# Fifteen short loads in the load queue, between two pieces of W_down

## The chip, the cores and the metric

The kernel runs on one core of a Trainium2 chip. The time is device time in microseconds (us), the median of several runs. A core has five engines with instruction streams of their own: TensorE (PE, matrix products; its weight loads are shown apart as PEld), VectorE (DVE), ScalarE (ACT), GpSimd (POOL) and SyncE (SP). SP computes nothing here. It issues transfers, which 16 DMA engines carry out. A transfer signals its end through a semaphore.

## The reference

One decode step of a transformer block, for a batch of 4 with one token each, in bfloat16. `x` is 4 x 576.

```
h  = x + Attention(layernorm(x))
h2 = h + MLP(layernorm(h))

Attention: q = x @ wq                     32 heads of 128
           k, v = the last 4096 rows of the caches, 16 heads (each serves 2 query heads)
           softmax(q k^T / sqrt(128)) v, then @ wo
MLP:       gate = x @ W_gate; up = x @ W_up      (576 x 4608)
           (gate where gate > 0) * up, then @ W_down   (4608 x 576)
```

Nearly all bytes are the K and V windows (128 MiB); the weights are another 24 MB.

## The kernel before, in words

The program is written as a list of operations per engine (`Prog`, `P.op`, `P.dma`); each names the operations it depends on, and `emit` turns these into semaphore waits. Each engine's list is executed in the order in which it was written.

All large loads are issued by SP, in one queue. `place` puts a load into a region of one SBUF tile (`arena`) and makes it wait for the readers of what was there before. The order is: `wq`; the K and V tiles, 16 of each, 4 MiB each, in a ring of four slots; `wo`; `W_gate` in two pieces; `W_up` in three; and `W_down` in five pieces (line 282). `WD_ROWS` = 0, 15, 25, 32, 35, 36 are the borders of these: W_down is held as 36 rows of 576 on each of 128 partitions, and piece 1 has rows 0 to 14, piece 2 rows 15 to 24, piece 3 rows 25 to 31, piece 4 rows 32 to 34, and piece 5 row 35. So a partition gets 17280, 11520, 8064, 3456 and 1152 bytes.

The K and V phase transposes each K tile on DVE (line 422), multiplies it with q on PE (lines 446 and 34), takes the softmax, and multiplies with V (lines 507 and 34). Then follow `wo`, the second layer norm, gate and up (line 664), and the product with W_down (line 685), which runs through the 36 rows in order, waiting for a piece where it begins. The result is copied out of PSUM by DVE (line 701) and ACT (line 702), and stored by two small transfers, one from SP and one from ACT (line 706). SP's last operation waits for both.

The regions of the five W_down pieces were used by K and V tiles; the last reader of these is a product with V, after which SP can issue all five.

Of the kernel before, what the change touches and what calls it, by code (L numbers as in the profile page):

```python
# [9 lines left out]
BF16 = mybir.dt.bfloat16  # L10
# [110 lines left out]
def bass_sequential_preLN__sliding_block_cached__glu_gated_reglu__decode_kernel(  # L121
# [12 lines left out]
    with ExitStack() as es:  # L134
        cnt = [0]

        def sb(name, shape, dt):
            return es.enter_context(nc.sbuf_tensor("sb_" + name, shape, dt))

        P = Prog()  # L140
# [48 lines left out]
        st2 = sb("st2", [128, 40], FP32)  # L189
        tmp5 = sb("tmp5", [128, DC, B], FP32)  # L190
        out_sb = sb("out_sb", [128, 352], BF16)


        pT = pp[:, 0:4096]
# [21 lines left out]
        def place(name, off, size, reader, make, key=None):  # L216
            deps = []
            for blk in range(off // 64, (off + size) // 64):
                r = owner.get(blk)
                if r is not None and r not in deps:  # L220
                    deps.append(r)
                owner[blk] = reader
            semk = key or "d_" + "_".join(str(v) for v in name)
            P.dma("sync", ("L",) + name, make, semk, deps)
            land[name] = off
# [19 lines left out]
        def main_rows(W):  # L245
            return W[0:512, :].rearrange("(p r) n -> p (r n)", r=4)
# [22 lines left out]
        for g, W in ((0, B_W_gate), (1, B_W_up)):  # L269
            for m, n, src in ((4, F // 2, last_rows(W)), (0, 3 * F, main_rows(W)[:, 0:3 * F]), (3, F, main_rows(W)[:, 3 * F:4 * F])):  # L270
                if g == 0 and m == 0:
                    n, src = 4 * F, main_rows(W)
# [7 lines left out]
        for r0, r1 in zip(WD_ROWS, WD_ROWS[1:]):  # L280
            place(("wd", r0), wd_off + r0 * D, (r1 - r0) * D, ("DOWN", 1),
                  lambda e, r0=r0, r1=r1: e.dma_start(  # L282
                      out=arena[:, wd_off + r0 * D:wd_off + r1 * D],
                      in_=B_W_down.rearrange("(p r) n -> p (r n)", p=128)[:, r0 * D:r1 * D]))


        pool("c_eps", lambda e: e.memset(eps_c[:, :], EPS))
# [15 lines left out]
                                                in_=c_qm[:, :, :].rearrange("p q (h j) -> p q h j", j=4),  # L303
# [4 lines left out]
                                                in_=to_v[:, :, :].rearrange("p n (k a) -> p n k a", a=4),  # L308
# [14 lines left out]
        for sg in range(2):  # L323
            pool(f"c_toq{sg + 1}", lambda e, sg=sg: e.affine_select(
                out=toq[:, :, :, :], in_=toq[:, :, :, :],
# [213 lines left out]
        def finish_o():  # L539
            for q in range(4):  # L540
                for qd in range(4):
# [17 lines left out]
                                              in_=bass.AP(tensor=e8, offset=0, ap=[[8, 128], [0, 4], [1, 8]])), ["c_e8", "c_selc0"])  # L559
# [47 lines left out]
        for a in range(8):  # L607
            for n in range(2):
                for j in range(4):
# [4 lines left out]
                    else:  # L614
# [6 lines left out]
                                             in_=bass.AP(tensor=psb, offset=512 + 224, ap=[[4096, 128], [1, 64], [0, 2]])), ["part1"])  # L621
# [54 lines left out]
        for i in range(2):  # L676
            dve(("HHT", i), lambda e, i=i: e.transpose(
                out=hhT[:, 576 * i:576 * i + 576].rearrange("p (r q) -> p r q", q=32),
                in_=bass.AP(tensor=pp, offset=3712 + 18 * i, ap=[[PPW, 128], [1, 18], [36, 32]])), [("HH", m) for m in range(3)])
# [24 lines left out]
        for n in range(2):  # L704
            lo, hi = ncol[n]
            P.dma(("sync", "scalar")[n], ("O", n), lambda e, n=n, lo=lo, hi=hi: e.dma_start(
                out=orow[:, lo:hi], in_=out_sb[32 * n:32 * n + 4, 0:hi - lo]),
                "d_out", [f"OUT{n}"])
        P.op("sync", None, None, [("O", n) for n in range(2)])
        P.emit(nc, es)  # L710


# [26 lines left out]
```

## Time and profile before

| | |
|---|---|
| time, median of 3 runs | 378.55 us (377.77 to 378.62) |
| profiled execution, span from the first to the last instruction | 376.5 us |
| what the median has above that span | 2.05 us |
| DVE busy | 227.6 us (60%) |
| PE busy | 209.2 us (56%) |
| read from HBM | 159.58 MB, 424 GB/s over the span |
| W_down pieces issued | 337.4 to 339.6 us |
| first product with W_down | 367.0 us |
| mean granted clock of TensorE | 0.791 |

The profiled execution has no time of its own beside its span, so the median is used for what lies around the span. A page of the profile shows the busy share of each engine in 40 equal slices of the span as digits (9 is 90% or more), the rows of the DMA queues (packets, MB, and the share of 16 engines' time), and the chain of work that ended last, followed back from the last instruction. In a timeline, a row has its start, its length, the engine, the line of the kernel, the operation, its output and inputs, and in brackets how long the engine had been idle and what ended that. The trace also has a record for every packet that a DMA engine moved, with its start, its duration and its size; a packet of 4 bytes is a write to a semaphore.

### The profile page before, as it was taken

The page shows a single profiled execution, that of the slowest core. Times are in us where ns is not written, and L with a number is a line of the kernel's source. Part 1 is how long each engine was busy: PE and PEld are TensorE (multiplying, and loading weights), DVE is VectorE, ACT ScalarE, POOL GpSimd, SP SyncE. Part 2 cuts the span into 40 slices and gives each one's busy share as a digit, 9 for nine tenths or more (in the row PEclk, how much of TensorE's full clock was granted, in tenths as well). Part 3 has the DMA queues.
Part 4 walks back from the last instruction along what each step waited for, and adds up shares of the span by engine and source line. Part 5 has one row for each costly group of instructions (what it writes and reads, how often), then busy time and mean ns, then how long its engine had stood idle before and what let it go on. Part 6 is the DMA issues. An engine that isn't in the chain of part 4 may idle for free.

```text
span 376.5 us, 2541 instructions
## 1 busy us (share of the span) xinstructions
PE 209.2 (56%) x1447; PEld 39.2 (10%) x694; DVE 227.6 (60%) x164; ACT 53.8 (14%) x84; POOL 10.7 (3%) x29
## 2 busy tenths in 40 slices
PE   0404443249919091749282844664555687776748
PEld 0000000001101010101010100110000101003305
DVE  3088878779292959584847778665659423342140
ACT  3093000211000114010101140101010401121010
POOL 8300000000000000000000000000000000000000
PEclk9975666659979687788778885968596989996688
DMA  8999999999999999999999999999999999999996
GB/s 335 446 435 432 413 446 446 425 411 446 444 421 414 443 444 421 414 446 446 421 413 446 446 418 421 438 446 418 425 439 446 413 432 435 430 423 426 437 414 263
DMA packets 6514, 159.74 MB, mean 424 GB/s; under 512 B 736, under 2 KB 872, under 8 KB 1512
## 3 DMA queue, kind: packets, MB, share of 16 engines
q1 hardware_dynamic: 6488, 159.58, 98.8%
q8 instruction: 8, 0.13, 0.1%
q10 hardware_dynamic: 16, 0.01, 0.0%
q14 instruction: 2, 0.02, 0.0%
HBM read 159.58 MB, written 0.00 MB: 424 GB/s over the span
## 4 chain that ended last, share of the span: by engine, by line
DMA 62%; DVE 18%; PE 18%; SPq 1%; issue 1%; ACT 0%
DMA sb_arena<-in_A_k_cache_dram 53%; DVE sb_arena L422 16%; PE psb L34 11%; DMA sb_arena<-in_B_W_down_dram 9%; PE psb L446 4%; PE psb L507 2%; DVE sb_o_tmp L520 1%; DVE sb_pp L485 1%; PE psb L685 0%; SPq L242 0%; PE psb L473 0%; SPq L282 0%; ACT sb_out_sb L702 0%; SPq L255 0%; SPq L251 0%
## 5 line engine op out<-in xcount | busy, mean ns | idle before, releaser
L422 DVE STREAM_TRANSPOSE sb_arena<-sb_arena 128x8192 f32<-128x8192 f32 (+1 forms) x19 | 139.9, 7365 | 66.5 <-DMA sb_arena<-in_A_k_cache_dram 66.5
L446 PE MATMUL psb<-sb_arena 128*32 128x512 bf16 x256 | 42.5, 629 | 119.1 <-DVE sb_arena L422 119.0
L34 PE MATMUL psb<-sb_arena,sb_pp 128*128 128x512 bf16 x382 | 105.2, 383 | 2.7 <-issue 2.6
L507 PE MATMUL psb<-sb_arena,sb_pp 128*128 128x512 bf16 x115 | 44.1, 383 | 8.9 <-DVE sb_o_tmp L520 8.9
L34 PE MATMUL psb<-sb_arena 128*32 128x512 bf16 x256 | 44.2, 649 | 0.0
L517 ACT COPY sb_o_tmp<-psb 32x512 f32<-32x512 f32 x32 | 18.5, 577 | 179.3 <-PE psb L34 179.1
L520 DVE TENSOR_TENSOR sb_o_tmp<-psb,sb_fm 32x512 f32<-32x512 f32 x32 | 21.7, 678 | 16.9 <-PE psb L34 16.4
L446 PEld LDWEIGHTS psb<-sb_arena 128*32 128x32 bf16 x256 | 9.6, 119 | 161.4 <-DVE sb_arena L422 132.2
L507 PEld LDWEIGHTS psb<-sb_arena,sb_pp 128*128 128x128 bf16 x128 | 12.6, 99 | 113.4 <-issue 113.4
L524 DVE TENSOR_REDUCE sb_o_sel<-sb_o_tmp 128x128 f32<-128x512 f32 x16 | 17.7, 1106 | 0.5
L465 ACT ACTIVATE sb_pp<-psb,sb_hx 128x1024 bf16<-128x1024 f32 x4 | 4.5, 1113 | 78.4 <-DVE sb_hx L462 78.4
L485 DVE TENSOR_TENSOR sb_pp<-psb,sb_m 128x1024 bf16<-128x1024 f32 x8 | 9.4, 1209 | 4.5 <-PE psb L473 4.5
L480 ACT ACTIVATE sb_pp<-psb,sb_m 128x512 bf16<-128x512 f32 x16 | 9.7, 692 | 14.8 <-PE psb L473 14.8
L523 DVE TENSOR_TENSOR sb_o_tmp<-sb_o_tmp,sb_fm 64x512 f32<-64x512 f32 x16 | 11.0, 690 | 0.5
L413 ACT COPY sb_arena<-sb_q_keep 32x256 bf16<-32x256 bf16 x8 | 9.7, 1452 | 0.1
L685 PE MATMUL psb<-sb_arena,sb_pp 128*32 128x352 bf16 (+1 forms) x72 | 7.6, 349 | 3.7 <-DMA sb_arena<-in_B_W_down_dram 3.6
L399 DVE CAST sb_pp<-psb 128x512 bf16<-128x512 f32 x1 | 2.4, 2426 | 11.3 <-PE psb L379 11.3
L468 DVE STREAM_TRANSPOSE sb_pp<-sb_pp 128x1024 bf16<-128x1024 bf16 x4 | 5.0, 1246 | 5.1 <-ACT sb_pp L465 5.1
L473 PE MATMUL psb<-sb_pp,sb_to_v 128*32 128x256 bf16 x64 | 4.3, 401 | 6.2 <-DVE sb_pp L468 6.2
L673 DVE TENSOR_TENSOR sb_pp<-psb,sb_pp 128x384 bf16<-128x384 f32 x3 | 1.5, 551 | 9.0 <-PE psb L664 9.0
L379 PE MATMUL psb<-sb_arena,sb_xnT 128*32 128x512 bf16 x16 | 2.6, 628 | 7.2 <-DMA sb_arena<-in_A_wq_dram 7.2
L664 PE MATMUL psb<-sb_arena,sb_hnT 128*32 128x384 bf16 x40 | 4.2, 405 | 3.9 <-DVE sb_hnT L645 2.0
(119 smaller groups left out, 88.1 us busy)
## 6 DMA issues: line engine op xcount, KB each, us to landing
sb_arena<-in_A_k_cache_dram SPq DMA_DIRECT2D x16, 4096.0 KB, 26.2
sb_arena<-in_A_v_cache_dram SPq DMA_DIRECT2D x16, 4096.0 KB, 28.5
sb_arena<-in_A_wo_dram SPq DMA_DIRECT2D x1, 4608.0 KB, 26.2
sb_arena<-in_B_W_gate_dram SPq DMA_DIRECT2D x1, 4608.0 KB, 29.3
sb_arena<-in_A_wq_dram SPq DMA_DIRECT2D x1, 4096.0 KB, 12.9
sb_arena<-in_B_W_up_dram SPq DMA_DIRECT2D x1, 3456.0 KB, 30.3
sb_arena<-in_B_W_down_dram SPq DMA_DIRECT2D x1, 2160.0 KB, 29.6
sb_arena<-in_B_W_down_dram SPq DMA_DIRECT2D x1, 1440.0 KB, 32.6
```

What stands on the lines that cost most here:

```text
L34: return e.add_instruction(mybir.InstMatmult(name=e.bass.get_next_instruction_name(), engine=mybir.EngineType.PE, ins=[e.lower_ap(rhs), e. ...
L413: act("QW", lambda e, i=i, q=q: e.copy(out=bass.AP(tensor=arena, offset=32 * i * AW + 2 * i + q, ap=[[AW, 32], [512, 16], [136, 4], [32, 4]]),
L422: dve(("TRA", g), lambda e: e.transpose(out=dst, in_=src), [("L", "K", g)] if lo == 0 else [])
L446: fn = lambda e, out_=out_, lhsT=lhsT, rhs=rhs, start=start, stop=stop: e.matmul(out_, lhsT=lhsT, rhs=rhs, start=start, stop=stop, skip_gr ...
L480: act(("EV", b, 0), lambda e, a=a: e.activation(out=bass.AP(tensor=pp, offset=2 * a, ap=[[PPW, 128], [8, 2], [32, 128], [1, 2]]), in_=bank ...
L485: dve(("EV", b, 1), lambda e, n=n: e.tensor_tensor(out=bass.AP(tensor=pp, offset=16 + 8 * n, ap=[[PPW, 128], [32, 128], [2, 4], [1, 2]]), ...
L507: fn = lambda e, lhsT=lhsT, rhs=rhs, k=k, j=j: e.matmul(bank[2 + j], lhsT=lhsT, rhs=rhs, start=(k == 0), stop=(k == 7), skip_group_check=True)
L517: act(("OSC", g), lambda e, j=j: e.copy(out=o_tmp[32 * j:32 * j + 32, 0:512], in_=bank[2 + j][32 * j:32 * j + 32, :]), [("PV", g), ("OSEL" ...
L520: dve(("OSD", g), lambda e, j=j: e.tensor_tensor(out=ot(32 * j, 32), in0=bank[2 + j][32 * j:32 * j + 32, :].rearrange("p (t d) -> p t d", ...
L523: dve(("OS", g), lambda e: e.tensor_tensor(out=ot(64, 64), in0=ot(64, 64), in1=fmb(64, 64), op=ALU.mult), [("OSC", g)])
L524: dve(("OSEL", g), lambda e: e.tensor_reduce(out=o_sel[:, qd, b, :], in_=o_tmp[:, 0:512].rearrange("p (t d) -> p d t", d=DH), axis=AX.X, o ...
L685: return lambda e: e.matmul(bank[n][32 * n:32 * n + 32, 0:hi - lo], lhsT=lhsT, rhs=w[:, lo:hi], start=start, stop=stop, skip_group_check=True)
```

## The change

After the load of the piece that begins at row 15, SP issues fifteen more loads. Load k takes the first 40 + k elements (bfloat16) of the first k rows of `wq`, and writes them to k partitions, eight apart, of a new scratch tile, `mark`. Nothing reads that tile. All fifteen count on one semaphore, and SP's last wait also waits for the fifteenth. The three remaining pieces of W_down are issued after them.

```
         out_sb = sb("out_sb", [128, 352], BF16)
+        mark = sb("mark", [128, 1024], BF16)
...
         for r0, r1 in zip(WD_ROWS, WD_ROWS[1:]):
             place(("wd", r0), ...)
+            if r0 == 15:
+                for k in range(1, 16):
+                    P.dma("sync", ("L", "mark", k), lambda e, k=k: e.dma_start(
+                        out=bass.AP(tensor=mark, offset=64 * k, ap=[[8 * 1024, k], [1, 40 + k]]), in_=A_wq[0:k, 0:40 + k]), "d_mark")
...
-        P.op("sync", None, None, [("O", n) for n in range(2)])
+        P.op("sync", None, None, [("O", n) for n in range(2)] + [("L", "mark", 15)])
```

## The prediction

> **What bounds the kernel now.** I read the page first, for the engines and the DMA row.
>
> ```profile
> span 376.5 us, 2541 instructions
> ...
> DMA  8999999999999999999999999999999999999996
> GB/s 335 446 435 432 413 446 446 425 411 446 444 421 414 443 444 421 414 446 446 421 413 446 446 418 421 438 446 418 425 439 446 413 432 435 430 423 426 437 414 263
> ...
> q1 hardware_dynamic: 6488, 159.58, 98.8%
> ...
> q10 hardware_dynamic: 16, 0.01, 0.0%
> ```
>
> The DMA engines are busy in all 40 slices, and 98.8% of their time belongs to q1, the queue that SP fills. No compute engine is busy for more than 60% of the span. So the time is that of 159.58 MB through one queue, and a change matters if it lengthens what stands in q1 or lets q1 run dry. Next, the chain of work that ended last, cut to the end, shows what follows the last bytes:
>
> ```profile
> 338.19 0.04 issue
> 338.23 34.60 DMA sb_arena<-in_B_W_down_dram
> 372.83 0.04 issue
> 372.88 1.86 PE psb L685 x19
> 374.74 0.02 issue
> 374.76 0.44 ACT sb_out_sb L702
> ```
>
> The third W_down piece is issued at 338.23 and lands at 372.83. Its 34.6 us are almost all waiting behind older transfers. After it come 1.86 us of PE and a copy. The timeline of the same stretch has the waits:
>
> ```profile
> 337.39 2.23 SPq L282 DMA_DIRECT2D sb_arena<-in_B_W_down_dram  x5
> ...
> 372.88 0.86 PEld L685 LDWEIGHTS psb<-sb_arena,sb_pp 128*32 128x32 bf16 x14 [0.48 <-DMA sb_arena<-in_B_W_down_dram]
> 373.95 0.45 PEld L685 LDWEIGHTS psb<-sb_arena,sb_pp 128*32 128x32 bf16 x8 [0.21 <-DMA sb_arena<-in_B_W_down_dram]
> 374.62 0.38 DVE L701 CAST sb_out_sb<-psb 32x224 bf16<-32x224 f32 x1 [8.34 <-PE psb L685]
> 374.76 0.44 ACT L702 CAST sb_out_sb<-psb 32x352 bf16<-32x352 f32 x1 [15.56 <-PE psb L685]
> 375.03 0.34 SPq L706 DMA_DIRECT2D out_dram<-sb_out_sb  x1
> ```
>
> SP issues all five pieces in 2.23 us. PE waits 0.48 us for piece 3 and 0.21 us for piece 4. Whatever delays the arrival of piece 4 delays the end by as much. Last, the list of issues:
>
> ```profile
> sb_arena<-in_B_W_down_dram SPq DMA_DIRECT2D x1, 2160.0 KB, 29.6
> sb_arena<-in_B_W_down_dram SPq DMA_DIRECT2D x1, 1440.0 KB, 32.6
> ...
> sb_arena<-in_B_W_down_dram SPq DMA_DIRECT2D x1, 1008.0 KB, 34.6
> ...
> sb_arena<-in_B_W_down_dram SPq DMA_DIRECT2D x1, 432.0 KB, 35.2
> sb_arena<-in_B_W_down_dram SPq DMA_DIRECT2D x1, 144.0 KB, 35.1
> ```
>
> Every piece waits about 30 us: the backlog at that point.
>
> **The change part by part.** The diff puts the fifteen loads behind the piece of rows 15 to 24, so they stand between the second and the third of the five pieces. Nothing is removed. PE, DVE, ACT and POOL keep their instructions in order. SP gets 15 issues and one wait.
>
> *Issue on SP.* The pieces follow one another at 0.47 us (2.23 us for five). Other rows for an issue are 0.33 us (the first piece, in the chain) and 0.56 us (the 4-row load of x on ACT). Fifteen cost 7.1 us, between 5.0 and 8.4. Piece 3 is then issued at 338.2 + 7.1 = 345.3 instead of 338.2, and piece 5 at 346.3. The trace's packet records show the first engine finishing its share of piece 2 at 368.2. The first load of the run was issued at 0.80 and had its first packet at 1.85, so 1.05 us are needed ahead. The cover is 368.2 - 1.05 - 346.3 = 20.8 us, and the issue costs nothing. Nobody else waits on SP: its next work is the output at 375.0. If this cover were gone, q1 would run dry ahead of piece 3.
>
> *Data in q1.* The loads have 1 + 2 + ... + 15 = 120 rows of 82 to 110 bytes, 12 KB together; by bytes alone, at 424 GB/s, 0.03 us. Per packet it is more. The packet records of the W_down pieces are straight in size:
>
> ```
> 3456-byte packets 135 ns, 1152-byte packets 51 ns (next one starts after 47),
> 4-byte semaphore packets 9 ns (next one starts after 6)
> ```
>
> That is 9 ns plus 0.0365 ns per byte, so a row takes 12 to 13 ns, of which 4 overlap with the next. A row and its semaphore packet add 8.5 + 6 = 14.5 ns to an engine's stream, or 21.5 without overlap. q10 in the page carried two transfers of 4 rows in 16 packets, 4 rows and 4 semaphore packets each, so I take one engine per row. Then one engine gets 15 rows, the next 14, and the last none. The longest stream grows by 15 x 14.5 = 0.22 us, at most 0.32. If instead some of these loads put all their rows on one engine, that engine has at most 120 x 8.5 + 15 x 6 = 1.1 us more.
>
> *Does it reach the end?* The engines finish unevenly: the semaphore packets of piece 2 lie between 368.19 and 369.99, ten of the sixteen in the last 0.63 us. If the busiest engine for these loads is a late one, the end moves by the full 0.22 us. If the six engines with the most rows are just the six early ones, a late engine still has up to 9 rows, 0.13 us. I take 0.2 us, between 0 and 1.1.
>
> *The last wait.* SP also waits for the fifteenth load, long landed. A step between SP instructions is 0.04 us in the chain; I take 0.04.
>
> *More code on SP.* Fifteen more instructions could fetch one more piece of code. Pieces of 16 KB took 1.0 to 1.1 us of one DMA engine in this trace while sharing it, about 0.6 us by its 27 GB/s (32768 bytes in 1.216 us). I take 0, bound 0.6, since SP has few instructions.
>
> *What the trace cannot show* is a dense row of small transfers in one queue. The nearest rows: pieces 4 and 5 are 1.08 and 0.38 us long per engine, and their packets stand without a gap. So a transfer does not wait for the one before it to be confirmed, at least at a spacing of 0.38 us. Confirmation takes longer than that: the last semaphore packet of piece 5 is at 373.85 and the semaphore is counted at 374.26, 0.41 us. A spacing of 15 ns is not shown by any row. So a load costs an engine 0.015 us if semaphore writes run on, and at most about 0.4 us if each waits for the one before. I take the low end, because no gap is there at 0.38 us, and keep 15 x 0.4 = 6 us as the high end. A gain has no source: packets already run at their fixed durations.
>
> Sum: 0 + 0.2 + 0.04 + 0 = 0.25 us. The page gives the profiled span, 376.5 us; the median of the timed runs, 378.55, lies 2.05 above it, and I leave that as it is. 378.55 + 0.25 = 378.8.
>
> **Rules of the Trainium skill against these rows.** "DMA: Bandwidth & Descriptors", Anatomy of one DMA, gives a fixed cost of about 2.0 us for every transfer, and its Rules for kernel authors say that transfers under 64 KB pay mostly overhead. Charged to the queue one by one that would be an estimated 15 x 2.0 = 30 us, the rule that speaks loudest against this change. The gapless pieces 4 and 5 say that the fixed part is latency and not occupancy, at their size. The same page calls the bubble of a semaphore write tiny, which sides with the 6 ns row. Its section on why a DMA increments its semaphore by 16 says that a transfer of k rows takes the lowest-numbered k engines; no row here shows which.
>
> **Rivals.**
> - *Confirmations line up (slower).* Fifteen semaphore writes stand close together on one engine, and each holds the next until it is confirmed. For: 0.41 us from packet to count, and no row with a closer spacing than 0.38 us. Against: no gap at 0.38 us. Price: up to 15 x 0.4 = 6 us on the engine with 15 rows; if that one is 1.4 us ahead of the last, 4.6. Time 383 to 384.5. A partial form (0.1 to 0.2 us each, a read that is not fetched far enough ahead) gives 1.5 to 3 us, 380 to 381.5. It decides from 0.08 us per load (1.14 / 15).
> - *The queue holds only so many transfers (slower).* At 339 nine transfers are outstanding and SP issues at its normal pace. With the change it would be 24. If there is a limit near 16, SP is held until small loads drain, after 370. Piece 3 then starts about 1.05 us late plus the issues of pieces 4 and 5, 2 x 0.47: 2.0 us, 380.6. Against: the nine are 81 descriptors per engine, without a stall; the fifteen add only 30 at most.
> - *Hidden altogether.* The early engines carry the rows and the late ones few: 0.05 us, 378.6. It can't be told from my forecast.
> - *Faster.* Only by chance, 377 or less; the runs before span 377.77 to 378.62.
>
> **How the numbers follow.** About 0.3%, 1.14 us, is what a measurement of this kernel can tell from no change. My forecast and the hidden case together, 378.5 to 379.1: 0.60. Confirmations in full: 0.15. Their partial form: 0.12. The limit of the queue: 0.09. A faster run: 0.04. The three slow cases sum to 0.36. The range begins at 377.9, below the hidden case by the spread of the runs, and reaches to 383.0, which takes in the partial form and the limit, and leaves out most of the full form. The likeliest case alone has 378.0 to 379.6.
>
> **What the profile after would show.** Right: q1 with 6488 + 240 = 6728 packets; SP issuing for some 9 us from 337.4; piece 3 with a landing time of about 27.7 us instead of 34.6, because it is issued 7 us later and lands at the same moment; PE's waits for pieces 3 and 4 changed by less than 0.3 us; the DMA row at 9 to the end. Wrong: a wait of PE for piece 3 that has grown from 0.48 us to several us, with the GB/s of slice 39 down (confirmations), or the issue of piece 3 after 360 (limit of the queue). Both would overturn the forecast. Fewer than 240 new packets would mean that rows do not go one to an engine.

## The result, and the profile after

| | before | changed |
|---|---|---|
| time, median of 9 runs | 378.31 us (377.77 to 378.62) | 379.21 us (378.88 to 379.49) |
| ratio | | 1.0024, 95% interval 1.0014 to 1.0034 |
| profiled execution, span | 376.5 us | 378.1 us |

The change costs 0.9 us. The time is inside the stated range, and the loss is within the 0.3% that the prediction called no change; but it is more than three times the 0.25 us of the forecast's sum, and the interval excludes that sum. The two profiled executions are 1.6 us apart, more than the medians. The one shown of before is near its fastest run: its span is 2.05 us below the median that was known then, while the changed kernel's profiled execution took 379.37 us with a span of 378.1, only 1.27 less. And piece 1 of W_down, which lands before any of the new loads has moved, already lands 0.27 us later in the changed kernel's profile (367.27 against 367.00); piece 2 lands 0.36 us later (370.77 against 370.41). That part is taken as a difference between executions.

The page of the changed kernel, engines and queue:

```profile
span 378.1 us, 2556 instructions
...
DMA  8999999999999999999999999999999999999995
GB/s 333 444 444 388 442 444 444 433 399 444 442 437 433 406 439 444 433 413 430 444 439 430 413 437 444 422 437 419 440 440 425 426 430 440 424 433 412 425 427 204
DMA packets 6754, 159.75 MB, mean 423 GB/s; under 512 B 976, under 2 KB 1112, under 8 KB 1752
...
q1 hardware_dynamic: 6728, 159.60, 98.6%
```

The queue has 240 packets more (6488 before), as worked out: 120 rows and 120 semaphore writes. The DMA engines count as busy to the end, so the loss does not show in the DMA row: a packet that is held up counts as a busy engine. The timeline at the end:

```profile
374.53 0.86 PEld L690 LDWEIGHTS psb<-sb_arena,sb_pp 128*32 128x32 bf16 x14 [1.17 <-DMA sb_arena<-in_B_W_down_dram]
...
375.59 0.46 PEld L690 LDWEIGHTS psb<-sb_arena,sb_pp 128*32 128x32 bf16 x8 [0.20 <-DMA sb_arena<-in_B_W_down_dram]
376.26 0.38 DVE L706 CAST sb_out_sb<-psb 32x224 bf16<-32x224 f32 x1 [9.70 <-PE psb L690]
376.40 0.44 ACT L707 CAST sb_out_sb<-psb 32x352 bf16<-32x352 f32 x1 [15.49 <-PE psb L690]
```

PE's wait for piece 3 has grown from 0.48 to 1.17 us; the one for piece 4 is unchanged (0.21, 0.20), and so is what follows. So the loss lies between the landings of pieces 2 and 3. Its chain there:

```profile
351.54 0.80 SPq L288
352.34 0.04 issue
352.38 22.10 DMA sb_arena<-in_B_W_down_dram
374.48 0.04 issue
374.53 1.85 PE psb L690 x19
```

From the landing of piece 2 to that of piece 3 it was 372.83 - 370.41 = 2.42 us; now it is 374.48 - 370.77 = 3.71, 1.29 us more in this execution. The busy times by stretch show when. The first table is of before, the second of the changed kernel. The last number of a row is what the DMA engines moved, in GB/s; ahead of it stand the DMA share and PE's granted clock:

```profile
368.00:370.00 2.00, 2.00 (x20) 1.25 (x17) 0.00 (x0) 0.00 (x0) 0.00 (x0) 0.50 0.98 416
370.00:372.00 2.00, 2.00 (x24) 1.28 (x22) 0.00 (x0) 0.00 (x0) 0.00 (x0) 0.81 0.99 412
372.00:374.00 2.00, 1.88 (x23) 1.12 (x21) 0.00 (x0) 0.00 (x0) 0.00 (x0) 1.00 0.55 213
```

```profile
368.00:370.00 2.00, 2.00 (x21) 1.40 (x17) 0.00 (x0) 0.00 (x0) 0.00 (x0) 0.50 1.07 363
370.00:372.00 2.00, 2.00 (x18) 1.00 (x16) 0.00 (x0) 0.00 (x0) 0.00 (x0) 0.50 0.99 326
372.00:374.00 2.00, 1.72 (x16) 0.87 (x13) 0.00 (x0) 0.00 (x0) 0.00 (x0) 0.89 0.83 329
```

From 368 to 372 the rate falls from 414 to 345 GB/s, while the DMA share stays near 1. (PE's wait grew by only 0.69 us, because PE itself came to piece 3 0.96 us later, at 373.36 instead of 372.40: it began 0.27 us later, and then needed 6.05 instead of 5.36 us for its weight loads of pieces 1 and 2, at a granted clock of 0.50 instead of 0.81 from 370 to 372.) The packet records say what holds the data up. They do not name the engine, so an engine's packets were strung together by their times, each beginning where the one before ends. The new rows are as fast as foreseen: 12 to 13 ns each, a row and its semaphore write every 14 to 15 ns. But of the 128 packets of piece 3 (8064 bytes, every one of them 305 ns before) 19 took more than 400 ns, up to 1576, always the first or the fifth of an engine's eight, and only on engines that had carried about five or more of the new loads. The large packets behind the new loads wait, not the new loads.

### The profile page after: what moved, and what is told of

Its sections match the earlier page's. It is cut to its first block, busy times and chain, and to the rows that moved or that the text cites. A ratio compares the mean times of both kernels' runs of the same rounds, so it can differ in the third digit from the quotient of the medians.

```text
span 378.1 us, 2556 instructions
## 1 busy us (share of the span) xinstructions
PE 210.9 (56%) x1447; PEld 38.7 (10%) x694; DVE 228.7 (60%) x164; ACT 53.8 (14%) x84; POOL 10.5 (3%) x29
## 4 chain that ended last, share of the span: by engine, by line
DMA 54%; PE 21%; DVE 20%; SPq 3%; issue 1%; ACT 0%
DMA sb_arena<-in_A_k_cache_dram 48%; DVE sb_arena L427 16%; PE psb L34 13%; DMA sb_arena<-in_B_W_down_dram 6%; PE psb L451 4%; PE psb L512 3%; SPq L288 3%; DVE sb_o_tmp L525 1%; DVE sb_pp L490 1%; PE psb L478 1%; PE psb L690 0%; DVE sb_pp L473 0%; DVE sb_hx L456 0%; ACT sb_pp L470 0%; SPq L283 0%
## 5 line engine op out<-in xcount | busy, mean ns | idle before, releaser
L34 PE MATMUL psb<-sb_arena,sb_pp 128*128 128x512 bf16 x382 | 107.8, 391 | 3.1 <-issue 3.0
L512 PE MATMUL psb<-sb_arena,sb_pp 128*128 128x512 bf16 x115 | 44.8, 390 | 8.9 <-DVE sb_o_tmp L525 8.9
L485 ACT ACTIVATE sb_pp<-psb,sb_m 128x512 bf16<-128x512 f32 x16 | 9.8, 697 | 14.5 <-PE psb L478 14.5
L34 PE MATMUL psb<-sb_arena,sb_hnT 128*32 128x384 bf16 x80 | 6.2, 394 | 0.0
```

The lines of the kernel that those rows point to most:

```text
L34: return e.add_instruction(mybir.InstMatmult(name=e.bass.get_next_instruction_name(), engine=mybir.EngineType.PE, ins=[e.lower_ap(rhs), e. ...
L485: act(("EV", b, 0), lambda e, a=a: e.activation(out=bass.AP(tensor=pp, offset=2 * a, ap=[[PPW, 128], [8, 2], [32, 128], [1, 2]]), in_=bank ...
L512: fn = lambda e, lhsT=lhsT, rhs=rhs, k=k, j=j: e.matmul(bank[2 + j], lhsT=lhsT, rhs=rhs, start=(k == 0), stop=(k == 7), skip_group_check=True)
```

## The experiments

Three theories were open: A, the engine reads ahead over a fixed number of packets, and short rows fill that; B, the semaphore writes at the end of the loads hold what stands behind them; C, SP is late with pieces 3 to 5. Every time below is compared with before on the same chip, and edits are against the changed kernel. "Gap" is the time from the landing of piece 2 to that of piece 3 in the profile (2.42 us before).

| run | loads | per engine: rows, semaphore writes | ratio (95%) | gap |
|---|---|---|---|---|
| the change | 15 of 1 to 15 rows | 0 to 15 each | 1.0024 (1.0014 to 1.0034) | 3.71 us |
| e1 | the same, behind piece 5 | 0 to 15 each | 1.0000 (0.9992 to 1.0009) | 2.43 |
| e2 | 4 of 12 to 15 rows | up to 4 each | 0.9999 (0.9990 to 1.0008) | 2.39 |
| e3 | 2 of 128 rows | 16, 2 | 1.0008 (0.9999 to 1.0017) | 2.55 |
| e4 | 15 of 16 rows | 15, 15 | 1.0062 (1.0050 to 1.0075) | 4.80 |
| e5 | 15 of 1 row | 15, 15 on one engine | 1.0009 (1.0000 to 1.0019) | 3.00 |
| e6 | 8 of 16 rows | 8, 8 | 1.0017 (1.0008 to 1.0026) | 3.04 |
| e7 | none; W_down in single rows | - | 1.0002 (0.9993 to 1.0011) | - |
| e8 | 15 of 16 rows among the K and V tiles | 15, 15 | 1.0084 (1.0071 to 1.0097) | 2.42 |
| e9 | 15 of 16 rows, from ACT's queue | 15, 15 | 1.0006 (0.9997 to 1.0015) | 2.60 |
| e10 | 15 of 16 rows, in five groups | 15, 15 | 1.0001 (0.9992 to 1.0010) | 2.46 |

### e1: the loads behind everything

```
-            if r0 == 15:
+            if r0 == 35:
```

> The fifteen loads stand behind the last piece of W_down instead of behind the second. Theory A (read-ahead: the engine reads ahead over a fixed number of packets; the short rows fill it, and the large packet behind them waits for its own read) and theory B (the fifteen semaphore writes hold what stands behind them) both put the cost on the 8064-byte packets behind the loads. Nothing stands behind them here: ratio 1.000 to before (0.999 to 1.001), all 8064-byte packets at 305 ns. If the cost is that of issuing fifteen loads on SP, or of having them anywhere in the program, the ratio stays at 1.0024.

The ratio is 1.0000, and every 8064-byte packet took 305 ns. The end of its chain is that of before, shown ahead, to 0.01 us:

```profile
338.23 34.60 DMA sb_arena<-in_B_W_down_dram
372.88 1.86 PE psb L690 x19
```

Fifteen issues on SP behind all the pieces (22.7 us of them here), the added code and the added wait cost nothing that shows. The cost is tied to what comes behind the loads: that it waits in the queue, or that SP issues it late, which this run undoes as well. Run e5 tells these two apart.

### e2: four loads

```
-                for k in range(1, 16):
+                for k in range(12, 16):
```

> Only the loads of 12, 13, 14 and 15 rows are left, so an engine has at most four rows and four semaphore writes. In the changed kernel engines with up to four loads kept 305 ns for every packet of piece 3. Theory A: 8 short packets are within the read-ahead, cost 4 x 15 ns = 0.06 us, ratio 1.000. Theory B with a price per semaphore write: 4/15 of the 0.9 us, 0.24 us, ratio 1.0006. Theory C (SP issues pieces 3 to 5 too late): SP is done some 8 us earlier, ratio 1.000.

Ratio 0.9999: four small loads, 54 rows in all, cost nothing that shows. The largest wait was 0.16 us, on a fifth packet. A fixed price per load is not supported, but its 1.0006 lies inside the interval.

### e3: the same packets with few semaphore writes

```
-                        out=bass.AP(tensor=mark, offset=64 * k, ap=[[8 * 1024, k], [1, 40 + k]]), in_=A_wq[0:k, 0:40 + k]), "d_mark")
+                        out=bass.AP(tensor=mark, offset=64 * k, ap=[[1024, 128], [1, 40 + k]]), in_=A_wq[0:128, 0:40 + k]), "d_mark")
```

(and k only 14 and 15.)

> Two loads of 128 rows of 108 and 110 bytes: 16 rows but only 2 semaphore writes on every engine, and two issues on SP instead of fifteen. Theory A counts packets, 18 per engine, like an engine with nine of the fifteen loads: about 1.0 us of waiting on the first and fifth 8064-byte packet plus 0.15 us for the rows, on every engine, the late ones too: piece 3 about 1.1 us later, ratio 1.003. Theory B counts semaphore writes, two: 0.15 us, ratio 1.0004. Theory C: SP issues as before, 0.15 us, ratio 1.0004.

Every engine has 16 short rows, more than any had in the change, but two semaphore writes. No 8064-byte packet took over 359 ns, and the gap is 2.55 us, 0.13 more than before: about the 0.15 of the packets themselves. Theory A, in packets, is out.

### e4: fifteen on every engine

```
-                        ... ap=[[8 * 1024, k], [1, 40 + k]]), in_=A_wq[0:k, 0:40 + k]), "d_mark")
+                        ... ap=[[8 * 1024, 16], [1, 40 + k]]), in_=A_wq[0:16, 0:40 + k]), "d_mark")
```

> All fifteen loads have 16 rows, so every engine has what only the first had: 15 rows and 15 semaphore writes. Theory A and B: the waiting of the engine with fifteen loads, 1.27 us on the first 8064-byte packet and 0.34 us on the fifth, and 0.22 us for the packets, on the late engines too: 1.8 us later, ratio 1.0048. If the cost came from uneven engines, ratio 1.0006 (0.22 us).

Ratio 1.0062, 2.3 us, somewhat above the 1.8 expected. The first packet of piece 3 took 1.55 to 1.99 us on all engines that could be followed in the records, the fifth 0.77 to 1.13. PE waits for piece 3 as long:

```profile
375.48 0.86 PEld L690 LDWEIGHTS psb<-sb_arena,sb_pp 128*32 128x32 bf16 x14 [2.63 <-DMA sb_arena<-in_B_W_down_dram]
375.48 1.85 PE L690 MATMUL psb<-sb_arena,sb_pp 128*32 128x224 bf16 x22 [2.27 <-DMA sb_arena<-in_B_W_down_dram]
```

The change is cheaper because its engines are uneven. The sizes of the rows tell the engines apart there: the eight that run late carried one to ten of the loads, and those that carried eleven or more, with three others, run early. The late engine with ten loads took 796 ns for its first packet of piece 3 and 1036 for its fifth, 1.22 us too much, and 0.15 for the ten rows and their writes: 1.37, where the gap grew by 1.29.

### e5: fifteen on one engine

```
-                        ... ap=[[8 * 1024, k], [1, 40 + k]]), in_=A_wq[0:k, 0:40 + k]), "d_mark")
+                        ... ap=[[8 * 1024, 1], [1, 40 + k]]), in_=A_wq[0:1, 0:40 + k]), "d_mark")
```

> All fifteen loads have one row, so one engine has 15 rows and 15 semaphore writes and the other fifteen engines have none. Theory B (semaphore writes that follow closely drain one by one, and large packets behind them wait): 8064-byte packets are stretched on one engine alone, to about 1.3 to 1.6 us for the first and 0.6 to 1.0 us for the fifth; if that engine is one of the six that run 1.4 us ahead, the end moves by 1.6 + 0.2 - 1.4 = 0.4 us, ratio 1.001, otherwise by 1.8, ratio 1.0048. Theory C (SP's slow issue, 10 us for fifteen loads, leaves pieces 3 to 5 late or in the way of the engines): fifteen issues as before, so all engines are stretched and the ratio stays near 1.0024.

Two 8064-byte packets of 128 are long, 1584 and 872 ns, the first and fifth of one engine; all others stay at about 305 ns. Theory C is out: SP issues fifteen loads here too, is held for 8.1 and 2.7 us at pieces 4 and 5 and done with them no sooner than in the change (357.5 in both), and fifteen engines see nothing of it. Piece 3 is issued 6 us earlier here than in the change, since a load of one row takes SP only 0.3 us; but there too it is issued (352.38) 16 us before its first packet (368.59), and engines with few loads show no stretched packet. The ratio, 1.0009, is about the 0.4 us expected of an early engine.

With one engine alone, the records show both sides of a semaphore write: when the engine wrote it, and when the semaphore counted it, in us:

```
semaphore packets of the 15 loads   368.712 368.726 368.740 368.754 ... 368.903 368.918
counts of their semaphore           369.350 369.535 369.720 369.905 ... 371.790 371.975
```

The packets go out every 14 to 15 ns; the counts come every 0.184 to 0.192 us. Semaphore writes that follow one another this closely are counted one at a time, about 0.185 us each. The large packet behind them begins at 368.924 and takes 1.58 us. Less its own 0.305 it could go on at about 370.2, when five of the fifteen were counted. The fifth, from about 371.42 for 0.87 us, could go on at 371.99, 0.02 us after the last count. So the large packets appear to wait for the counts. Whether a semaphore write takes the 0.185 us by itself, or waits for the row ahead of it to be written, no run here shows: in every run whose packets waited, each of these semaphore writes has a short row directly ahead of it.

### e6: eight on every engine

```
-                for k in range(1, 16):
+                for k in range(8, 16):
```

(with 16 rows each, as in e4.)

> Eight loads of 16 rows: 8 rows and 8 semaphore writes on every engine. Theory B, from the engine with eight loads in the changed kernel (first packet 0.11 us longer, fifth 0.78): 0.9 us of waiting and 0.12 us of packets on the late engines, ratio 1.0027. If the waiting were in proportion to the count, 8/15 of the 2.3 us of the run with fifteen loads of 16 rows: 1.2 us, ratio 1.003. Theory C: half the issues, ratio half of 1.0062, 1.003; this run doesn't tell C from B, its first packets do: near 305 ns by B.

First packets took 0.37 to 0.50 us, fifth ones 0.72 to 1.10; ratio 1.0017, 0.64 us, less than the 1.0027 expected from single engines of the change. It is below proportion: eight cost 0.64 us, fifteen 2.3. So it seems that a few writes can be pending without holding data. From eight to fifteen a further write cost (2.3 - 0.64) / 7 = 0.24 us, an estimate for which the two intervals allow 0.13 to 0.36; 0.185 for the count and 0.015 for the packets would fit. By the counts of e5, fifteen writes are counted 0.64 (the first) + 14 x 0.185 = 3.2 us after the first was written, and e2's four would be 1.2 us after, which is what four packets of 0.3 us last. That fits e2, where the longest wait of a fifth packet was 0.16 us, but it is an argument and not a measurement.

### e7: small loads that are not close together

```
-        WD_ROWS = (0, 15, 25, 32, 35, 36)
+        WD_ROWS = (0, 15) + tuple(range(25, 37))
```

(against before; no added loads.)

> No extra loads: the last eleven rows of W_down come as eleven loads of one row each instead of three loads of 7, 3 and 1. Per engine a load is 8 packets of 1152 bytes, 0.38 us, and one semaphore write. Theory B: 0.38 us between semaphore writes is longer than the 0.2 us that one takes to drain, so nothing waits: packets stay at 51 ns, and PE can follow row by row, which ends up to 0.25 us sooner: ratio 0.9993 to 1.000. If each of eleven loads cost what one of the fifteen does (0.06 to 0.15 us): ratio 1.002 to 1.004.

All 1408 packets of 1152 bytes took 51 ns: eleven semaphore writes per engine at a spacing of 0.38 us hold nothing. Ratio 1.0002. The small gain that had been thought possible did not come: PE does follow row by row, but eight packets of 1152 bytes take 0.38 us where a row's share of the larger packets is 8 x 301 / 7 = 0.34, so the last row is counted 4.11 us after piece 2 instead of 3.85.

### e8: in the middle of the attention

```
         for g in range(NTILE):
             add_kv("K", g)
+            if g == 8:
+                (the fifteen loads of 16 rows)
```

> Fifteen loads of 16 rows stand between a K tile and a V tile in the middle of the attention, far from the end. Theory B: the queue is the bound there too, the 32768-byte packets behind the loads wait as the 8064-byte ones did, about 2.1 us, and all that follows in the queue moves: ratio 1.0062, as with the same loads behind piece 2. If the stream makes up the loss, or only the tail is sensitive, ratio 1.000 to 1.001.

Ratio 1.0084: the loss isn't made up, and is larger than at the end. The stretches of this run around the loads:

```profile
135.00:140.00 5.00, 5.00 (x24) 0.59 (x6) 3.05 (x6) 1.21 (x2) 0.00 (x0) 1.00 1.09 372
140.00:145.00 5.00, 2.78 (x25) 0.46 (x17) 2.49 (x1) 2.60 (x5) 0.00 (x0) 1.00 0.63 220
145.00:150.00 5.00, 0.00 (x0) 0.00 (x0) 5.00 (x4) 1.29 (x3) 0.00 (x0) 0.74 1.01 433
```

Before had 449 and 419 GB/s in the first two of these stretches. The difference, (449 - 372) x 5 + (419 - 220) x 5 = 1380 KB, is 3.2 us at 430 GB/s, all of the loss (0.0084 x 378 = 3.2). Here the rows themselves were spread, up to 0.2 us apart, and 32 KB packets ahead of the loads were held too (2.3 us instead of 1.2). Why the same loads cost about 1 us more among 32 KB packets was not tried.

### e9: from another queue

```
-            if r0 == 15: (the loads, in SP's list)
+        for k in range(1, 16):
+            P.dma("scalar", ...)      (16 rows each, in ACT's list behind the activations of gate)
```

> The fifteen loads of 16 rows are issued by ACT, in its own queue, after its three activations of gate, while ACT has nothing to do. Theory B (a semaphore write takes 0.185 us on its engine, one after the other, as the counts of the run with one-row loads showed): ACT needs some 0.6 us for an issue, so an engine never has two of these writes at hand, nothing waits, and 0.22 us of packets remain: ratio 1.0006, against 1.0062 for the same loads in SP's queue. If any fifteen small loads in the last 40 us cost the same: 1.006.

Ratio 1.0006, no 8064-byte packet over 322 ns. The result is the one expected, but not for the reason given there. ACT had issued all fifteen loads by 368.25, when only 105 of their 240 rows had moved, so the engines did have several of the semaphore writes at hand. The packet records show what kept these apart: an engine moved one packet of ACT's queue and one of SP's in turn, so that a large packet stood after each row and each semaphore write. Two semaphore writes of the loads were 1.3 us apart among the packets of 17280 bytes, 0.87 among those of 11520, and 0.62 among those of 8064; only among the small packets of pieces 4 and 5 did they come as close as about 0.15.

### e10: the same loads in groups of three

```
                 place(("gu", g, m), ...)
+                if g == 1 and m in (0, 3): (three loads of 16 rows)
...
-            if r0 == 15: (fifteen loads)
+            if r0 in (0, 15, 25): (three loads of 16 rows)
```

> The same fifteen loads of 16 rows in SP's queue, but in five groups of three, behind the second and third pieces of W_up and the first three of W_down. Theory B: a group with the semaphore write of the piece before it is 4 x 0.185 = 0.74 us of draining, and the run with four loads showed waits of 0 to 0.16 us for that; the next group comes 1 us or more of data later: 0.22 us for the packets and up to 0.5 us of waits, ratio 1.0006 to 1.002, against 1.0062 for the same fifteen together. If each load has a fixed price wherever it stands, 1.0062.

Ratio 1.0001, against 1.0062 for the same 240 rows and 240 semaphore writes in one stretch of the same queue, and no 8064-byte packet over 313 ns. The end of its chain:

```profile
346.67 26.64 DMA sb_arena<-in_B_W_down_dram
373.31 0.04 issue
373.35 1.83 PE psb L696 x18
```

## Why the prediction was right, and where it was off

- *What bounds the kernel*: right. Piece 2 landed 0.36 us later and piece 3 a further 1.29, and the span grew by about their sum, 1.6; e8 shows far from the end that a loss in q1 is not made up.
- *Issue on SP*: the size was wrong, the conclusion right. Fifteen issues took 11.3 us (341.06 to 352.34), 0.75 each, above the upper bound of 8.4; the last pieces were then held for 1.8 and 2.7 us. The rows 0.33 and 0.56 were too narrow a base: one after the other, loads of one row took 0.3 us each (e5) and loads of 16 rows 0.63 (e4). Piece 5 was on its way at 357.5, still 10 us before even the first packet of piece 3 had to be issued (368.59 - 1.05), and e5 shows that it cost nothing.
- *Data in q1*: right for the packets' own time (14.5 ns predicted, 14 to 15 measured; 240 packets).
- *Does it reach the end?* This is the step that failed: its 0.2 us used the low price of *What the trace cannot show*, "a load costs an engine 0.015 us if semaphore writes run on, and at most about 0.4 us if each waits for the one before". They are counted one by one, 0.185 us apart (e5). The low end was taken because pieces 4 and 5 stand without a gap at a spacing of 0.38 us; that row could show only that such a write holds nothing at this spacing. The price came to 2.3 us with fifteen on every engine (e4), and to 0.9 us with the uneven fifteen of the change, against 0.2 in the sum.
- *The rival "confirmations line up"* named the mechanism; in its partial form it gave 1.5 to 3 us, and put the point from which it decides at 0.08 us per load. It came to 0.9 / 15 = 0.06 us per load, just on the other side. The evenly loaded e4 cost 2.3 / 15 = 0.15 per load, which is the partial form and well below the 0.4 of the full one.
- *The queue holds only so many transfers*: SP was held, but the cost of 2 us did not follow, since what is held in SP stands behind a full queue. In e7 one issue was held for 9.9 us without effect. Nor is the limit one of 16 transfers: in e5, 22 were outstanding (six large loads, the fifteen and piece 3) before an issue was held.
- *The last wait and the code*: nothing that e1 could measure.
- *Luck*: the time came out close partly by chance. The base of 378.55 was the median of three runs, and that of nine is 0.24 lower, which hid part of the 0.65 us that the sum was short; and the five engines that carried eleven or more of the loads were early ones. With fifteen on the late engines too, in e4, the loss was 2.3 us.
- *The signs to look for*: the wait of PE for piece 3 had been named as the sign of this rival, and it grew by 0.69 us, more than the 0.3 that the forecast allowed and less than the "several us" that were to overturn it. Piece 3 took 22.1 us from issue to landing and not 27.7: SP could begin with W_down only at 340.22, 2.8 us later than before, behind the last product with V, and its issues took 4.2 us longer than foreseen.

The Trainium skill ("DMA: Bandwidth & Descriptors", Anatomy of one DMA) gives the fixed cost of about 2.0 us for transfers that GpSimd issues, and puts it down mostly to the completion of a transfer; the loads here are issued by SP. Charged to the queue, as the prediction tried, it does not hold: e10 had fifteen loads for nothing that shows. The same section calls the bubble of a semaphore write tiny. That agrees with the 6 ns that one takes in the stream, and fails here for a run of fifteen (e4, 2.3 us). The page's statement (Queues, rings and completion order) that a semaphore increment lands only after every earlier write of its engine would fit the 0.185 us of e5, though no run here shows that this is what the time is spent on.

## What to carry to other kernels

When a row shows that something does not wait at one spacing, it says nothing about closer spacings: here "no gap at 0.38 us" was compatible with 0.185 us for each, and fifteen in a row cost 2.3 us. In a queue that is the bound, count the transfers per engine that stand close together, not their bytes: four short loads in a row cost nothing that could be measured, eight 0.6 us, fifteen 2.3, and the same fifteen in threes between large transfers, or from a queue of their own, again nothing that could be measured. And look for the price of a small transfer in the large packets behind it, since its own records look innocent and the DMA share stays near 1.

## What the runs showed of the hardware that was not expected

- Semaphore writes that one DMA engine wrote 14 to 15 ns apart were counted about 0.185 us apart (e5: fifteen counts between 369.350 and 371.975).
- The large packets behind wait at the first and the fifth, not evenly (e4: 1.55 to 1.99 and 0.77 to 1.13 us, the six others at 0.305 with few exceptions). Why these two is open.
- With loads of two queues at hand, a DMA engine moved a packet of each in turn, which kept the semaphore writes apart (e9: 0.62 us among 8064-byte packets).
- An issue on SP waits when the queue has much outstanding: in e7 the sixth piece of W_down took 5.5 us to issue and a later one 9.9, where 0.43 is normal; before, with nine transfers outstanding, none waited. It is not the number of transfers alone, since 22 were outstanding in e5 before one waited; what is counted was not settled.
- A load of k short rows took k engines, one row on each (the packet count, and e5's one engine). The engines do not end together: in the profile of before the semaphore packets of piece 2 are 1.8 us apart between the first and the last engine, and in the changed kernel the five engines with eleven or more of the loads were all among the early eight.
